# An odd-width shift, earlier softmax weights for the first batch, and projection steps under the last attention tiles

## The chip, the cores and the metric

The kernel runs on one core of one Trainium2 chip. The metric is the time of one execution on the device, in microseconds (us).

## The reference

A thresholded attention feeds a two-layer network:

```python
# q, k, v: (8 batches, 8 heads, 576 positions, 64); tau = 0.02
scores = scale * q @ k^T
thresh = max(scores, axis=-1) - tau
scores = where(scores >= thresh, scores, -1e9)
attn   = softmax(scores)                      # per row
x      = (attn @ v) -> (4608 tokens, 512)     # heads side by side
h      = x @ w_in                             # 512 -> 2048
out    = (h - tanh(h)) @ w_out                # 2048 -> 512, fp32
```

## The kernel before

The 64 heads are taken as 32 pairs. A pair is cut into 9 tiles of 128 query rows: A, B, A, B for the first head, a middle tile M with the last 64 rows of both heads, and A, B, A, B for the second. That makes 288 tiles, and the program is one loop over 288 **slots**. In slot s it starts the scores of tile s + 8, shifts the maxima of tile s + 7, bends tile s + 5, makes the softmax weights of tile s and multiplies tile s − 2 with v. The network's steps for the block of 512 tokens before ("h" for hidden, "y" for projection) are dealt out over the slots. Block 6 and 7 end in a tail after the last slot.

The parts that the change touches:

```python
def scores(i):
    ...  # matmuls into ps (ps_big, 2 buffers)
    if kind(j) == "B":
        mx = mxs[i] = mxs.pop(i - 1)          # B writes column 1 of A's tile
    else:
        mx = mxs[i] = st_pool.tile([P, 2], F32, name="mx", tag="mx")
    c = int(kind(j) == "B")
    nc.vector.tensor_scalar(                  # scale, evict, and row maximum
        out=sc, in0=ps[:, lo : lo + S], scalar1=SC, scalar2=None,
        op0=ALU.mult, op1=ALU.max, accum_out=mx[:, c : c + 1])

def shift(i):                                 # nb = tau - max, for A and B at once
    kd = kind(i % TPP)
    if kd == "A":
        return
    n = 2 if kd == "B" else 1
    mx = mxs.pop(i)
    nb = st_pool.tile([P, 2], F32, name="nb", tag="nb")
    nc.vector.tensor_scalar(
        out=nb[:, 0:n], in0=mx[:, 0:n], scalar1=-1.0, scalar2=tau,
        op0=ALU.mult, op1=ALU.add)
    ...
# kink(i):    ScalarE, z = Prelu(sc + nb) with a steep negative side
# weights(i): first batch: TensorE transposes z, ScalarE takes exp; later by DMA transposes
# attend(i):  TensorE, weights times v

def q_by_dma(p):                              # q of these pairs is transposed by DMA
    return p >= 2 * HPAIR and p % 2 == 1

def y_step(m, ms, part):                      # in layers(m, tail)
    if part == 0:
        odd = ms % 2
        pl, tag = (ps_o, "o") if tail and odd else (ps_y, "y")   # one buffer each
        ys[m, ms] = pl.tile(...), odd
    ps, odd = ys[m, ms]
    project(m, ms, part, ps, tail and odd)    # odd rows are emptied by ScalarE
```

GpSimd (POOL in the profile) splits q and k into two fp16 halves (`khl`, `qhl`), copies v and the weights, and swaps the halves of k (`kS`). Each of these instructions takes 0.3 to 1.3 us in the trace before (group means 0.29 to 1.28).

## Time and profile before

| | before |
|---|---|
| time, median of 3 runs | 544.43 us (544.36 to 545.31) |
| span of the profiled run | 542.9 us |
| until slot 37 or so (8 to 64 us) | POOL, ACT and DVE all near full |
| 64 to 138 us | DVE and ACT near full |
| 138 to 470 us | PE 97% busy |
| tail (470 us to the end) | PE alone |

The page's first row gives each engine's busy us, share and count of instructions:

```profile
PE 507.5 (93%) x4722; PEld 290.3 (53%) x4790; DVE 447.1 (82%) x1196; ACT 439.3 (81%) x630; POOL 290.7 (54%) x390
```

PE leads, but it can't gain on itself: what moves the end is idle time of PE, and who causes it. The prediction shows the stretches and lines that tell this.

### The profile page before, as it was taken

Reading aid. Unit: us, or ns where it says so; the run is one execution under the profiler, and the core shown is the slowest. Engines: PE = TensorE matmul, PEld = TensorE weight load, DVE = VectorE, ACT = ScalarE, POOL = GpSimd, SP = SyncE. Lnnn points to the kernel's source line nnn. Section 1 sums busy time; section 2 is a strip of 40 time slices with the busy share of each in tenths; the row PEclk is TensorE's granted clock in tenths of the full one; section 3 lists DMA queues with packets and bytes.
Section 4 is the critical chain, followed back from the end, with each engine's and each line's share of the span. In section 5 each row is a group of like instructions: output and inputs, shape, how many; then the busy total and the mean of one; then the engine's idle time right before and its main releaser. Section 6 shows DMA issues by size and latency. Waiting matters only on the chain.

```text
span 542.9 us, 12962 instructions
## 1 busy us (share of the span) xinstructions
PE 507.5 (93%) x4722; PEld 290.3 (53%) x4790; DVE 447.1 (82%) x1196; ACT 439.3 (81%) x630; POOL 290.7 (54%) x390
## 2 busy tenths in 40 slices
PE   5888888889999899999999999999999999899997
PEld 3566655555555555555555555555555555444444
DVE  4999999898888899889988989989989988544440
ACT  4899999998898888889888989899888989633330
POOL 7899987765456666557555755666655730000000
PEclk9999999998999999999999999999999999999999
DMA  7554688679697988789988999999999965310103
GB/s 211 168 182 145 205 202 175 148 131 197 141 173 160 175 169 199 163 191 195 181 188 172 177 200 186 165 171 191 192 177 179 200 127 117 83 41 39 40 39 77
DMA packets 202239, 85.13 MB, mean 157 GB/s; under 512 B 169792, under 2 KB 194624, under 8 KB 202176
## 3 DMA queue, kind: packets, MB, share of 16 engines
q1 hardware_dynamic: 201584, 83.89, 72.7%
q8 instruction: 37, 0.61, 0.5%
q10 hardware_dynamic: 592, 0.43, 0.3%
q14 instruction: 26, 0.21, 0.1%
HBM read 36.70 MB, written 9.44 MB: 85 GB/s over the span
## 4 chain that ended last, share of the span: by engine, by line
PE 67%; DVE 19%; POOL 6%; ACT 4%; issue 3%; DMA 0%; ACTq 0%; SPq 0%; DVEq 0%; POOLq 0%
PE psY L504 19%; PE psH L478 17%; PE psS L313 14%; DVE sc L323 9%; PE psO L423 5%; DVE g L497 3%; PE psS L303 3%; PE ps_k L227 3%; PE psHt L478 3%; DVE nb L337 2%; ACT z L357 2%; DVE osb L438 1%; POOL kS L256 1%; PE ps_q L227 1%; PE psO L412 1%
## 5 line engine op out<-in xcount | busy, mean ns | idle before, releaser
L323 DVE TENSOR_SCALAR_CACHE_REDUCE sc<-psS 128x576 f32<-128x576 f32 x288 | 215.3, 749 | 16.4 <-PE psS L313 11.0
L357 ACT ACTIVATE z<-sc,nb 128x576 bf16<-128x576 f32 x256 | 194.2, 771 | 21.9 <-DVE nb L337 21.3
L256 POOL COPY kS<-kT 64x1152 f16<-64x1152 f16 x62 | 70.9, 1143 | 135.8 <-DVE nb L337 133.2
L504 PE MATMUL psY<-w_out_sb,g 128*128 128x512 bf16 (+1 forms) x556 | 138.4, 373 | 2.2 <-issue 0.8
L394 ACT ACTIVATE pT<-zT 128x1152 f16<-128x1152 bf16 (+1 forms) x128 | 137.3, 1073 | 0.0
L478 PE MATMUL psH<-xT,w_in_sb 128*128 128x512 bf16 x451 | 118.0, 379 | 6.5 <-DVE g L497 4.4
L313 PE MATMUL psS<-kT,qT 128*128 128x512 f16 (+1 forms) x512 | 105.6, 288 | 11.2 <-DVE sc L323 9.2
L491 ACT ACTIVATE th<-psH 128x512 f32<-128x512 f32 x128 | 75.5, 590 | 39.2 <-PE psH L478 37.0
L313 PEld LDWEIGHTS <-qT 128*128 128x128 f16 x1024 | 73.1, 98 | 61.3 <-issue 14.5
L497 DVE SCALAR_TENSOR_TENSOR g<-th,psH 128x512 bf16<-128x512 f32 x128 | 87.2, 681 | 18.4 <-ACT th L491 18.4
L313 PE MATMUL psS<-kS,qT 128*128 128x512 f16 x496 | 101.9, 287 | 0.1
L478 PEld LDWEIGHTS <-w_in_sb 128*128 128x128 bf16 x576 | 49.4, 98 | 60.7 <-issue 7.2
L504 PEld LDWEIGHTS <-g 128*128 128x128 bf16 x592 | 51.0, 98 | 56.6 <-issue 2.9
L423 PEld LDWEIGHTS <-pT 128*128 128x128 f16 x1280 | 55.7, 98 | 25.0 <-issue 1.4
L423 PE MATMUL psO<-vb,pT 128*128 128x65 bf16 x1280 | 61.5, 194 | 0.9 <-ACT pT L394 0.6
L337 DVE TENSOR_SCALAR nb<-mx 128x2 f32<-128x2 f32 (+1 forms) x160 | 49.1, 307 | 2.5
L386 ACT ACTIVATE pT<-psZ 128x640 f16<-128x640 bf16 (+1 forms) x56 | 37.6, 671 | 5.1 <-PE psZ L377 5.0
L180 POOL TENSOR_TENSOR qhl<-qraw,qhl 128x576 f16<-128x576 f32 x31 | 39.7, 1281 | 2.6
L180 POOL TENSOR_TENSOR khl<-kraw,khl 128x576 f16<-128x576 f32 x31 | 39.7, 1281 | 2.6
L250 DVE COPY kT<-ps_k 128x1152 f16<-128x1152 f16 x31 | 23.4, 756 | 13.6 <-PE ps_k L227 13.2
L514 DVE COPY yo<-psY 128x512 f32<-128x512 f32 (+1 forms) x31 | 21.1, 679 | 11.3 <-PE psY L504 6.4
L438 DVE TENSOR_TENSOR osb<-psO,rc 128x256 bf16<-128x256 f32 x64 | 27.2, 424 | 2.2
(77 smaller groups left out, 508.4 us busy)
## 6 DMA issues: line engine op xcount, KB each, us to landing
vraw<-in_v_dram SPq DMA_DIRECT2D x32, 256.0 KB, 3.4
out_dram<-yo SPq DMA_DIRECT2D x32, 256.0 KB, 3.0
kraw<-in_k_dram SPq DMA_DIRECT2D x31, 256.0 KB, 3.2
qraw<-in_q_dram SPq DMA_DIRECT2D x31, 256.0 KB, 3.6
wt<-in_moe_w_in_dram SPq DMA_DIRECT2D x8, 512.0 KB, 4.7
wt<-in_moe_w_out_dram SPq DMA_DIRECT2D x8, 512.0 KB, 4.1
zT<-z SPq DMA_TRANSPOSE x104, 3.5
kraw<-in_k_dram SPq DMA_DIRECT2D x32, 32.0 KB, 2.8
```

Source lines behind the costliest of these rows:

```text
L180: nc.gpsimd.tensor_tensor(out=hl[:, :, 1, :], in0=x, in1=hl[:, :, 0, :], op=ALU.subtract)
L256: nc.gpsimd.tensor_copy(out=o, in_=i)
L313: nc.tensor.matmul(out=ps[:, dst], lhsT=lhs, rhs=kk[:, src], start=(n == 0), stop=(n == 1),)
L323: nc.vector.tensor_scalar(out=sc, in0=ps[:, lo : lo + S], scalar1=SC, scalar2=None, op0=ALU.mult, op1=ALU.max, accum_out=mx[:, c : c + 1],)
L337: nc.vector.tensor_scalar(out=nb[:, 0:n], in0=mx[:, 0:n], scalar1=-1.0, scalar2=tau, op0=ALU.mult, op1=ALU.add,)
L357: nc.scalar.activation(out=z, in_=sc, func=ACT.Prelu, bias=nb, scale=1.0, alpha=STEEP)
L394: nc.scalar.activation(out=pt[:, 0 : n * P], in_=zts.pop(i)[:, 0:n, :], func=ACT.Exp)
L423: nc.tensor.matmul(out=po[:, (j - 1 - 5 * hh) + ab, :], lhsT=pt[:, blk * P : (blk + 1) * P], rhs=vb[:, hh, c, :], start=(n == 0), stop=(n ...
L478: nc.tensor.matmul(out=ps, lhsT=w_in_sb[:, c, n * P : (n + 1) * P], rhs=xs[m][:, c, :] if m < B else xR[:, c, :, :], start=(c == 0), stop= ...
L491: nc.scalar.activation(out=th, in_=ps, func=ACT.Tanh)
L497: nc.vector.scalar_tensor_tensor(out=gs[m][:, n, :], in0=th, scalar=-1.0, in1=ps, op0=ALU.mult, op1=ALU.add,)
L504: nc.tensor.matmul(out=ps, lhsT=gs[m][:, n, ms * P : (ms + 1) * P], rhs=w_out_sb[:, n, cols], start=(n == 0), stop=(n == DF_C - 1),)
```

## The change

Its intent, as I read it: an element count of 3 in place of 2 should keep the shift from waiting for GpSimd. In the trace before, a shift of 128x2 takes 0.16 to 0.17 us where GpSimd is idle and up to 1.27 us where it starts inside a GpSimd instruction, and those over 230 ns end within 0.04 us of the end of one; this wait is called the lock below. For this the maxima move to six fixed tiles with a third, constant column. The weights of the first 36 tiles run four slots sooner. The q of pair 30 is transposed by DMA. Three projection steps of block 6 run in the three slots after the last one, where PE waits for the last attention tiles; odd rows of block 6 then share the other rows' accumulator, since the second one is still in use. The diff is cut; left out are lines that follow from these, and one in `ready` for block 0, which never asks it and so is not changed.

```diff
+    mx3 = []
+    for i in range(6):
+        mx = const.tile([P, 3], F32, name=f"mx{i}")
+        nc.vector.memset(mx, 0.0)
+        mx3.append(mx)
...
-        return p >= 2 * HPAIR and p % 2 == 1
+        return p >= 2 * HPAIR and (p % 2 == 1 or p == 30)
...
-            mx = mxs[i] = st_pool.tile([P, 2], F32, name="mx", tag="mx")
+            mx = mxs[i] = mx3[i // 2 % len(mx3)]
...
-        n = 2 if kd == "B" else 1
+        n = 3 if kd == "B" else 1
-        nb = st_pool.tile([P, 2], F32, name="nb", tag="nb")
+        nb = st_pool.tile([P, 3], F32, name="nb", tag="nb")
...
+    FIRST = 3
...
                 odd = ms % 2
+                odd = odd and m >= B - 1
...
                 not now or not ready(now[0]) or len(at) * ahead <= i * 16
-            ):
+            ) and not (m == B - 1 and i < FIRST):
...
+    for i in range(NTILE + 3):
+        at = i - 4 if i < HPAIR * TPP else i
+        atts.setdefault(at + LAG, []).append(i)
+        if i < NTILE:
+            wts.setdefault(at, []).append(i)
...
+        if s == NTILE:
+            todo = layers(stage, True)
+            share, done, stage = 1, 0.0, stage + 1
...
-        if 0 <= s < NTILE:
-            weights(s)
+        for i in wts.pop(s, []):
+            weights(i)
+        if 0 <= s < NTILE + FIRST:
...  (attend, norm and emit_x follow atts in the same way; the steps left over run after the loop)
```

More of the change, by code (lines that the diff above doesn't have):

```diff
@@ L340, in shift @@
         )
-        nbs[i] = nb[:, n - 1 : n]
+        nbs[i] = nb[:, n // 2 : n // 2 + 1]
         if kd == "B":
@@ L572, in ready @@
             last = 4 * y[2] + 3
-            return y[0] < m or len(at) > last and at[last] + 2 < i
+            return y[0] < m or len(at) > (last if m else 15) and at[last] + 2 < i
         while now or len(at) < 16:
@@ L658 @@
             plan.setdefault(-AHEAD, []).extend(plan.pop(at))
-    kinks = {}
-    for i in range(NTILE):
-        kinks.setdefault(i // 2 * 2 + 2 - AHEAD if i < 4 else i - MASK, []).append(i)
+    kinks, wts, atts = {}, {}, {}
+    for i in range(NTILE + 3):
[3 more added lines that the diff above has]
+            wts.setdefault(at, []).append(i)
+            kinks.setdefault(i // 2 * 2 + 2 - AHEAD if i < 4 else i - MASK, []).append(i)
     for s in range(-AHEAD, NTILE + LAG + 3):
@@ L679 @@
         bend()
-        if 0 <= s < NTILE:
-            weights(s)
+        for i in wts.pop(s, []):
+            weights(i)
+        if 0 <= s < NTILE + FIRST:
             if todo:
                 done += share
-                if j == TPP - 1 and p % HPAIR == HPAIR - 1:
+                if s < NTILE and j == TPP - 1 and p % HPAIR == HPAIR - 1:
                     done = 1e9
@@ L696 @@
         del stores[:-1]
-        if 0 <= s - LAG < NTILE:
-            attend(s - LAG)
-            pp, jj = divmod(s - LAG, TPP)
-            if jj == 4:
-                norm(pp, 0)
-            if jj == 8:
-                norm(pp, 1)
-        pp, jj = divmod(s - LAG, TPP)
-        if jj == 1 and 0 < pp <= NPAIR:
-            emit_x(pp - 1)
+        for i in atts.pop(s, []):
+            pp, jj = divmod(i, TPP)
+            if i < NTILE:
+                attend(i)
+            if i < NTILE and jj in (4, 8):
+                norm(pp, int(jj > 4))
+            if jj == 1 and pp:
+                emit_x(pp - 1)
         for step in plan.pop(s, []):
@@ L715 @@
                     w_load(piece)
+    for step in todo:
+        step()
+        bend()
+        shrink()
+        for store in stores:
+            store()
+        stores.clear()
     while stage < NMB:
```

## The prediction

If the lock is dodged, 6.4 + 0.2 + 0.6 − 0.4 = 6.8 us less than 544.4, thus 537.6 us; if not, without the 6.4, 0.4 us less, thus 544.0 us.

> **What bounds the kernel now.** I read the page first, then the stretches of the trace by busy time, then the chain of waits, then single lines. The program has no single bound, so I cut it into stretches. The columns are the stretch in us, its length, then busy us (and instructions) of PE, PEld, DVE, ACT and POOL, the granted clock, the DMA share and GB/s:
>
> ```profile
> 8.00:64.00 56.00, 49.19 (x651) 34.74 (x649) 51.08 (x145) 48.83 (x80) 52.10 (x65) 1.00 0.59 181
> 64.00:138.00 74.00, 65.27 (x714) 40.88 (x721) 68.39 (x183) 67.64 (x101) 54.24 (x69) 0.98 0.81 168
> 138.00:470.00 332.00, 323.03 (x3006) 180.72 (x3057) 297.36 (x817) 296.69 (x408) 178.81 (x229) 1.00 0.88 174
> 470.00:543.00 73.00, 67.37 (x341) 32.27 (x343) 27.77 (x44) 23.15 (x39) 0.00 (x0) 1.00 0.14 44
> ```
>
> From 138 us on PE is busy 323.03 of 332 us: only PE work, or its 9 us of idle time, can be won there. From 64 to 138 us DVE (68.39 of 74) and ACT (67.64) are near full together. Before 64 us POOL is as full as DVE, and the chain of waits stays on POOL from 37.3 to 73.3 us. Three of its pieces (start, us, what), and the wait of PE that proves POOL the limit in this stretch:
>
> ```profile
> 61.01 1.04 POOL w_out_sb L605
> 62.11 1.15 POOL kS L256
> 63.30 1.16 POOL kS L256
> ```
>
> ```profile
> 37.33 1.28 POOL L180 TENSOR_TENSOR qhl<-qraw,qhl 128x576 f16<-128x576 f32 x1
> 38.67 0.68 PE L227 MATMUL ps_q<-ident_f,qhl 128*128 128x128 f16 x9 [1.10 <-POOL qhl L180]
> ```
>
> The q transposes start 0.06 us after POOL ends qhl. I paired every POOL product with its first use on PE: the slack is 0.06 to 0.54 us for the k and q of head pairs 2 to 5, and the kS of pair 5 ends at 64.44 us where PE uses it. It is 2.9 us and more for pair 6 and later. POOL's gaps from 17 to 73 us are the 40 to 90 ns between any two of its instructions. So up to 64 us the clock of the program is POOL's work list, which the change does not shorten.
>
> Now the line that the change aims at. The two groups of the shift (count | busy us, mean ns | idle before), then two places where it ran long:
>
> ```profile
> L337 DVE TENSOR_SCALAR nb<-mx 128x2 f32<-128x2 f32 x128 | 44.4, 347 | 2.5
> L337 DVE TENSOR_SCALAR nb<-mx 128x1 f32<-128x1 f32 x32 | 4.6, 144 | 0.0
> ```
>
> ```profile
> 122.31 1.28 POOL L180 TENSOR_TENSOR khl<-kraw,khl 128x576 f16<-128x576 f32 x1
> 122.34 1.27 DVE L337 TENSOR_SCALAR nb<-mx 128x2 f32<-128x2 f32 x1
> ...
> 274.58 1.28 POOL L180 TENSOR_TENSOR qhl<-qraw,qhl 128x576 f16<-128x576 f32 x1
> ...
> 274.85 1.03 DVE L337 TENSOR_SCALAR nb<-mx 128x2 f32<-128x2 f32 x1
> ...
> 277.80 1.02 PE L478 MATMUL psH<-xT,w_in_sb 128*128 128x512 bf16 x4 [0.67 <-DVE g L497]
> ```
>
> Two elements per partition cost 1.27 and 1.03 us, and each ends within 0.03 us of the end of the POOL instruction beside it. I went through all 160: every 128x2 one over 230 ns does so, the rest lie at 142 to 230 ns, and no 128x1 one is ever long, even when it starts inside a POOL instruction. The last line shows what it can cost: the first hidden-layer matmul of a block waits 0.67 us because the copies ahead of its operand on DVE were late.
>
> [...] the trace holds no odd width but 1 and can't say. This is my largest doubt. [...] the large sc evictions, which read PSUM, do last about 0.75 us with or without POOL at work beside them.
>
> **The change part by part.**
> 1. Odd width (2 becomes 3, the maxima in six fixed tiles). If it dodges the lock, 128 × (347 − 144) = 26.0 us of DVE waiting goes. By stretch, from busy time of that line less 144 ns each: 8.54 − 24 × 0.144 = 5.1 us before 64 us; 10.89 − 27 × 0.144 = 7.0 us from 64 to 138; 29.62 − 111 × 0.144 = 13.6 us from 138 to 470. Before 64 us POOL paces the program, so I count 0.4 us (the one real POOL gap, 1.04 us at 16.2 us, waits for a DVE copy that stands behind a 0.63 us shift). From 64 to 138 us the 7.0 us leave DVE at 61.4 busy, and ACT with 67.6 of 74 becomes the next bound: I count 3 us. From 138 us most of it becomes DVE idle time. PE's waits there for DVE are 3.0 (psH for g) + 1.6 (psS for sc) + 0.5 (xT) + 0.2 = 5.3 us; I count 3 us. Sum 6.4 us. Six more memsets at about 0.1 us lie in the first 4 us, where DVE waits for the first load.
> 2. Softmax weights four slots sooner for the first 36 tiles: nothing is added or removed. Four exponentials of about 0.6 us (0.612 and 0.716 mean) move into ACT's idle time at 13.9, 17.4 and 19.0 us (1.04, 1.45 and 0.82 us), so ACT, which lags by about 3 us until 40 us, leads sooner. But POOL paces these slots and slot 37 comes at 64 us either way. The first hidden-layer step comes at the same slot. I count 0.2 us.
> 3. q of pair 30 turned by DMA: 9 transposes leave PE, 20.64 us / 279 = 0.074 us each, 0.67 us, in a stretch where PE sets the pace; I count 0.6 us. A DVE copy of 0.75 us goes too. The DMA takes about 3.4 us to land, and DMA load falls just there because loads end.
> 4. Three projection steps (12 matmuls, 3 × 0.86 us) under the last attention tiles. PE idles there now:
>
> ```profile
> 470.79 0.49 PE L423 MATMUL psO<-vb,pT 128*128 128x65 bf16 x10 [0.57 <-ACT pT L394]
> ...
> 472.02 0.40 PE L455 MATMUL psX<-ident_bf,osb 128*128 128x128 bf16 x4 [0.74 <-DVE osb L438]
> ```
>
> These 1.3 us would be filled. Against it: block 6 now keeps one accumulator tile, where odd rows had another one, and ACT to empty it. The first two steps meet at a row change at once, a wait for the copy of about 0.85 us (0.69 us and the handing over). Later at three row changes one hidden step of 0.86 us stands between, while DVE first finishes g (0.69) and then copies yo (0.69): some 0.4 us each. Sum: 1.3 − 0.85 − 1.2 = −0.7; some overlap is likely, so I count −0.4 us.
>
> If the lock is dodged: 6.4 + 0.2 + 0.6 − 0.4 = 6.8 us less, 537.6 us. If not: 0.4 us less, 544.0 us.
>
> **Rivals.** (a) [...] Then the shift stays at about 350 ns and the time at 544. [...] Against it: a width of 1 is never held, and such care for a width (a third, constant column) makes sense only if it works. I give it 35%. (b) The lock goes, but ACT or the DMA transposes take over at once: ACT is at 91% from 64 to 138 us, and one PE wait of 1.46 us at 122.1 us is for a q transpose by DMA. Then only 3 us come, 541. (c) The held DVE was the hidden pacemaker: each hold also delays evictions, and so PE, beyond the named waits (nb holds 10 us, 1.9%, of the chain of waits), and the sooner weights help more than I allow. Then 10 to 12 us, 533. (d) The single accumulator costs more than the filled idle time: 1 us more at the end.
>
> **Range and chances.** 65% at about 537.6 (535 to 541) and 35% at about 544 (543 to 545) put the middle near 538.5. Eight in ten: 533.5 to 544.8. Faster by over 2% means below 533.5 us, thus (c): 10%. Slower by 2% would need a new stall of 11 us, for which I see no source: 2%.
>
> **What would show it.** The shift's group as 128x3 with a mean near 150 ns (lock dodged) or near 350 (not). Slot 37, PE's first use of pair 5's kS, still at 64 us within 1 us. The stretch after it some 3 us shorter, with ACT fuller than DVE. The 0.67 us waits before psH gone. At the end, the two waits of 0.57 and 0.74 us gone and new waits of psY for the yo copy. I am wrong if the time to 64 us falls by more than 1 us, if the shift is short and the time stays above 541, or if PE's transposes or the loads get a new wait.

## The result

The kernel after takes 547.54 us (median of 6 runs, 546.08 to 547.75) against 544.65 us (6 runs) for the kernel before on the same chip. The ratio is 1.0046, with a 95% interval of 1.0032 to 1.0060. Ratios here are the mean time of one kernel's fast runs over that of the other's of the same rounds, so they are not quite the ratio of the medians quoted. The kernel is a little slower, outside the predicted range of 533.5 to 544.8 us.

The shift's groups in the kernel after (count | busy us, mean ns | idle before):

```profile
L343 DVE TENSOR_SCALAR nb<-mx 128x3 f32<-128x3 f32 x128 | 45.0, 351 | 2.4
L343 DVE TENSOR_SCALAR nb<-mx 128x1 f32<-128x1 f32 x32 | 4.6, 145 | 0.0
```

Three wide takes 351 ns on average where two wide took 347. The lock is still there. But that explains only why nothing was won, not a loss. The same stretches as before, and one longer at the end:

```profile
8.00:64.00 56.00, 50.39 (x670) 34.95 (x669) 52.48 (x150) 50.40 (x82) 52.99 (x66) 1.00 0.61 187
64.00:138.00 74.00, 65.12 (x714) 40.50 (x725) 67.30 (x184) 68.33 (x101) 56.08 (x72) 1.00 0.78 167
138.00:470.00 332.00, 318.38 (x2957) 177.49 (x3007) 297.08 (x806) 294.04 (x403) 176.86 (x226) 1.00 0.86 174
470.00:546.00 76.00, 70.02 (x357) 33.32 (x361) 30.62 (x50) 23.63 (x39) 0.00 (x0) 1.00 0.14 42
```

Fixed clock times compare different work once one kernel is ahead, so I cut the traces by work instead: from the first score eviction to the 91st ("head"), to the 280th ("body"), and from there to the end.

| profiled run | first eviction at | head | body | end | span |
|---|---|---|---|---|---|
| before | 8.52 us | 129.60 | 308.89 | 95.94 | 542.9 |
| after | 8.71 us | 127.08 | 313.45 | 96.52 | 545.8 |

The head is 2.5 us shorter, the end 0.6 us longer, and the body, which no part of the change was meant to touch, **4.6 us longer**. PE does the same work there (300.75 and 300.61 us busy within these bounds); its idle time grew. What PE waited for, in us in total, times, and the longest, from 138 us on: first before, then after (there to 473 us):

```profile
PE psH L478 <- DVE g L497: 3.0, 5, 0.7
...
PE psS L313 <- DVE sc L323: 1.6, 5, 0.7
...
PE psH L478 <- DVE xT L468: 0.5, 1, 0.5
```

```profile
PE psS L319 <- DVE sc L329: 4.6, 9, 1.3
PE psH L484 <- DVE g L503: 2.7, 5, 0.7
PE psH L484 <- DVE xT L474: 2.5, 5, 0.5
```

PE waits more for DVE. To find why, I followed DVE in step through both traces. Where both are in the same rhythm, a shift of the one stays at a constant distance from the same shift of the other, except at one place in each even head pair, where the kernel after loses 0.22 us. DVE at that place in pair 16, before and after:

```profile
238.97 0.14 DVE L337 TENSOR_SCALAR nb<-mx 128x1 f32<-128x1 f32 x1
239.03 0.75 DVE L323 TENSOR_SCALAR_CACHE_REDUCE sc<-psS 128x576 f32<-128x576 f32 x1
```

```profile
236.68 0.15 DVE L343 TENSOR_SCALAR nb<-mx 128x1 f32<-128x1 f32 x1
236.96 0.76 DVE L329 TENSOR_SCALAR_CACHE_REDUCE sc<-psS 128x576 f32<-128x576 f32 x1
```

The eviction that follows M's shift starts 0.06 us after the shift's start in the kernel before, and 0.28 us after it in the kernel after. The list of instructions says why. Columns: place, line, operation, tiles, engines waited for:

```
421 L343 TensorScalarPtr nb<-mx_99 128x1 [waits DVE_49]
422 L329 TensorScalarPtr sc,mx_99<-psS 128x576 [waits DVE_49,PE_49]
```

The two use one tile, mx_99. The new index is `i // 2`. In an even pair M is tile 4 and the next A is tile 5 of the pair, counted from an even number, so both give the same index. The eviction of A now writes into the tile that M's shift has just read, and must wait for that shift to end. The kernel after has 16 evictions with such a wait on their own engine, the kernel before none; in its trace they start 0.27 to 0.31 us after the start of M's shift in all 16 even pairs, against 0.06 us in 14 of them before.

Four slots later in the same pair, before and after, this is what the step does:

```profile
243.61 0.66 POOL L179 CAST khl<-kraw 128x576 f16<-128x576 f32 x1
...
244.18 0.17 DVE L337 TENSOR_SCALAR nb<-mx 128x2 f32<-128x2 f32 x1
...
244.36 1.28 POOL L180 TENSOR_TENSOR khl<-kraw,khl 128x576 f16<-128x576 f32 x1
```

```profile
242.07 1.28 POOL L186 TENSOR_TENSOR khl<-kraw,khl 128x576 f16<-128x576 f32 x1
242.14 1.23 DVE L343 TENSOR_SCALAR nb<-mx 128x3 f32<-128x3 f32 x1
```

Before, the shift starts 0.09 us ahead of the end of GpSimd's cast and is out after 0.17 us. After, it comes 0.07 us behind the start of the next, longer instruction and is held for 1.23 us. A step of 0.22 us became 1.06 us more.

At the tail, the waits of PE named in the prediction are gone and the feared ones are there: 0.78 us at the first row change, and three more of 0.28 us. The first of them:

```profile
474.11 1.02 PE L510 MATMUL psY<-w_out_sb,g 128*128 128x512 bf16 x4 [0.78 <-DVE yo L520]
```

### The profile page after: what moved, and what is told of

The parts are those of the page before. It is cut to its first block, busy times and chain, and to the rows that moved or that the text cites. A ratio compares the mean times of both kernels' runs of the same rounds, so it can differ in the third digit from the quotient of the medians.

```text
span 545.8 us, 12963 instructions
## 1 busy us (share of the span) xinstructions
PE 506.3 (93%) x4713; PEld 287.9 (53%) x4781; DVE 449.9 (82%) x1203; ACT 439.4 (81%) x628; POOL 291.0 (53%) x390
## 4 chain that ended last, share of the span: by engine, by line
PE 65%; DVE 23%; ACT 5%; issue 4%; DMA 2%; SPq 0%; DVEq 0%; ACTq 0%
PE psY L510 18%; PE psH L484 16%; PE psS L319 14%; DVE sc L329 11%; PE psO L429 5%; DVE g L503 4%; PE psS L309 3%; PE ps_k L233 3%; DVE nb L343 2%; ACT z L363 2%; PE psHt L484 2%; DVE yo L520 2%; ACT pT L392 2%; DVE osb L444 1%; PE psO L418 1%
## 5 line engine op out<-in xcount | busy, mean ns | idle before, releaser
L343 DVE TENSOR_SCALAR nb<-mx 128x3 f32<-128x3 f32 (+1 forms) x160 | 49.6, 310 | 2.4
L520 DVE COPY yo<-psY 128x512 f32<-128x512 f32 (+1 forms) x33 | 22.5, 680 | 12.1 <-PE psY L510 7.6
```

The lines of the kernel that those rows point to most:

```text
L343: nc.vector.tensor_scalar(out=nb[:, 0:n], in0=mx[:, 0:n], scalar1=-1.0, scalar2=tau, op0=ALU.mult, op1=ALU.add,)
```

## The experiments

My theory S: the shared tile of maxima costs the body its time, by itself and by moving DVE onto longer holds of GpSimd. Rivals: W, the width itself costs; N, the body's pattern is a matter of chance and any change in the head can upset it. For each run I give the time, the ratio to the kernel before of the same rounds, and the lengths from its one trace. The diffs are cut to the lines that matter. "Hold" is what shifts in the body last beyond 170 ns each, summed: 11.54 us before, 14.68 us after.

### p1_odd: part 1 alone, as in the diff

```diff
-            mx = mxs[i] = st_pool.tile([P, 2], F32, name="mx", tag="mx")
+            mx = mxs[i] = mx3[i // 2 % len(mx3)]
-        n = 2 if kd == "B" else 1
+        n = 3 if kd == "B" else 1
```

> The kernel before with part 1 alone, as in the diff (three-wide shift, maxima in six fixed tiles taken by i // 2). Theory S (the fixed tiles make the middle tile M and the next tile A of each even head pair share one tile of maxima, so that 16 evictions wait for the shift before them, 0.22 us each, and the DVE falls behind GpSimd by that step): slower, 546.5 to 549 us, 16 evictions with a DVE wait, body (138 to 470 us of before) some 3 to 5 us longer. Theory W (the width itself costs): slower too, but then the next run, p1_apart, is as slow. Theory N (the body depends on chance of timing from the head alone): same as before, 544.6.

548.56 us, ratio 1.0057 (1.0038 to 1.0075). Body 312.41 us, hold 13.58 us, 16 evictions with the wait. Part 1 by itself accounts for the whole loss (1.0046 in the kernel after); what the other parts win back is within the intervals.

### p1_apart: part 1 with a tile of its own for M

```diff
-            mx = mxs[i] = mx3[i // 2 % len(mx3)]
+            mx = mxs[i] = mx3[(5 * (i // TPP) + (j + 1) // 2) % len(mx3)]
```

> As p1_odd, but the six tiles are taken in turn by group, so that M and A never share one. Theory S: 544.6 us within 0.7, no eviction waits for a shift, the shift as 128x3 still about 350 ns mean (the lock stays). Theory W: as slow as p1_odd, 546.5 or more. If three wide dodged the lock after all, the mean would be near 150 ns and the time 538.

545.65 us, ratio 1.0007 (0.9994 to 1.0019): as before. (This is 1.0 us above the 544.6 expected, but the kernel before stood at 545.2 in these rounds.) Body 308.92 us, hold 11.53 us, no eviction with the wait. The same place in pair 16:

```profile
237.95 0.14 DVE L343 TENSOR_SCALAR nb<-mx 128x1 f32<-128x1 f32 x1
238.01 0.75 DVE L329 TENSOR_SCALAR_CACHE_REDUCE sc<-psS 128x576 f32<-128x576 f32 x1
```

The step back to 0.06 us takes the loss away with the width left at 3. W falls. The shift as 128x3 takes 346 ns here, so a width of 3 is neither a help nor a harm.

### p1_share2: the shared tiles, two wide

```diff
+        mx = const.tile([P, 2], F32, name=f"mx{i}")
-            mx = mxs[i] = st_pool.tile([P, 2], F32, name="mx", tag="mx")
+            mx = mxs[i] = mx3[i // 2 % len(mx3)]
```

> The kernel before with the six fixed tiles and their sharing, but the shift left two wide. Theory S: slower like p1_odd, within 0.7 us of it. Theory W: 544.6.

546.98 us, ratio 1.0035 (1.0016 to 1.0055). Body 311.08 us, hold 12.30 us. The sharing costs without the width. The time is 1.6 us below p1_odd's, where at most 0.7 us was expected; the two intervals overlap, so this gap is not shown to be a real one.

Where the body loses its time can be read pair by pair, from the start of M's shift against the same shift before. By the M of the next pair, each of the three kernels with the sharing has made the 0.22 us good within 0.04 us after the even pairs 10, 12, 14, 18, 22 and 26. The loss comes after pairs 16, 20, 24 and 28, where the kernel before has no long hold (none of its shifts there is over 0.31 us):

| | after pairs 16, 20, 24, 28 | sum | body longer by |
|---|---|---|---|
| p1_share2 | 0.53, 0.53, 0.53, 0.53 us | 2.1 | 2.2 |
| p1_odd | 0.52, 0.52, 0.54, 1.87 us | 3.4 | 3.5 |
| kernel after | 1.87, 0.54, 0.53, 1.87 us, and 0.40 won back after pair 29 | 4.4 | 4.6 |

With about 0.53 us one shift is held 0.67 to 0.68 us, with 1.87 us two are held 1.23 and 0.8 us, where each took 0.17 us before. So the waits as such cost the body next to nothing. They cost by moving shifts onto longer holds of GpSimd: S is right in its second half only. Which hold is met differs between kernels that share the tile alike, so N has a share in the size, but not in the cause.

### after_apart: the kernel after, with a tile of its own for M

The edit of p1_apart, on the kernel after.

> The kernel after, whole, but with the tiles of maxima taken by group (no sharing). Theory S: the body goes back to what before needs, and the 2.3 us won in the head stay: 542 to 544 us. Theory W or N: stays near 547.5 us.

543.98 us, ratio 0.9974 (0.9962 to 0.9986). Body 308.55 us, hold 11.60 us. One index takes the kernel after from 0.46% slower to 0.26% faster than before. So the shared tile is the cause of the loss in the whole kernel too, and not only in part 1.

### p2_sooner: the earlier weights alone

```diff
+        at = i - 4 if i < HPAIR * TPP else i
-            weights(s)
+        for i in wts.pop(s, []):
+            weights(i)
```

> The kernel before with the softmax weights of the first 36 tiles four slots sooner and nothing else. The head pair 5 starts its scores 2.0 us sooner in the kernel after (64.77 for 66.75 us), pair 10 2.3 us sooner. Theory S (the body's loss is from the shared tiles): 542.3 us, all of the head's gain kept. Theory N (any shift of phase in the head upsets the body): 544 to 547 us. My prediction's step (POOL paces the head, 0.2 us): 544.4 us.

543.8 us, ratio 0.9975 (0.9955 to 0.9994), so some 1.4 us less (0.3 to 2.5). That is more than the 0.2 us of the prediction, and less than the 2.3 us that S had expected (542.3 us). Body 308.83 us: N would have had the body upset by the part, and it is not. The head is 128.04 against 129.60 us, but this alone shows little: heads without the part differ by 1.3 us between traces (129.60 before, 128.26 in p1_share2). What the part changes in the head is shown at pair 5, below.

### p4_tail: the steps under the last attention tiles alone

```diff
+                odd = odd and m >= B - 1
+            ) and not (m == B - 1 and i < FIRST):
+        if s == NTILE:
+            todo = layers(stage, True)
```

> The kernel before with block 6's three projection steps under the last attention tiles and nothing else. From the trace of after: idle PE of 0.57 and 0.74 us goes, waits of psY for yo of 0.78 and 3 times 0.28 us come: 0.33 us slower, 545.0 us. If the filled time were worth more than the waits, faster.

545.91 us, ratio 1.0012 (0.9993 to 1.0031). By the trace, PE's waits of 0.57 and 0.74 us are gone, those of 0.78 and three of 0.28 us are there, and the end is 96.59 against 95.94 us, 0.65 us longer. The ends of the ten traces without the part lie between 95.87 and 95.95 us, those of the three with it between 96.52 and 96.61. So the part is a small loss in the traces, and unclear in the times.

### p3_q30: the q of pair 30 by DMA alone

```diff
-        return p >= 2 * HPAIR and p % 2 == 1
+        return p >= 2 * HPAIR and (p % 2 == 1 or p == 30)
```

> The kernel before with q of pair 30 turned by DMA and nothing else. 9 transposes less on PE, 0.67 us, in a stretch where PE is the bound: 544.0 us if nothing else moves; up to 1 us slower if the phase between DVE and GpSimd or the landing of the transpose upsets pairs 29 to 31.

544.67 us, ratio 0.9987 (0.9969 to 1.0004): unclear, at most a little faster. In its trace the body is 309.01 us, no shorter than before. PE's 0.67 us of transposes turned into a new wait of 0.66 us, at the first scores of pair 30:

```profile
431.83 0.36 PEld L313 LDWEIGHTS <-qT 128*128 128x128 f16 x4 [1.15 <-DMA qT<-qhl]
431.83 0.42 PE L313 MATMUL psS<-kT,qT 128*128 128x512 f16 x2 [0.66 <-DVE nb L337]
```

The view puts the matmul's wait down to a shift on DVE, which these scores don't use. Its weights wait for the transposed q: the DMA is issued at 428.43 us and lands at 431.79, and both instructions start 0.04 us later. So the wait is for the transpose itself.

### shift_ones: two shifts of one column

```diff
-        nc.vector.tensor_scalar(out=nb[:, 0:n], in0=mx[:, 0:n], ...)
+        for c in range(n):
+            nc.vector.tensor_scalar(out=nb[:, c : c + 1], in0=mx[:, c : c + 1], ...)
```

> The kernel before with the shift of two maxima done as two instructions of one column each. [...] no shift is over 200 ns and the 26 us of DVE waiting are replaced by 128 more instructions of 144 ns (18 us, less where they overlap). Lock theory: body's PE waits for DVE (0.67 us before psH once a batch, 0.2 us) go, and the time is 540 to 543 us. If the lock's cost lay off the critical path: 544.6 or slower, since DVE has more instructions.

538.61 us, ratio 0.9884 (0.9863 to 0.9904). This is the experiment that measures what the lock costs, in a kernel that does the same arithmetic:

```profile
L338 DVE TENSOR_SCALAR nb<-mx 128x1 f32<-128x1 f32 x288 | 35.7, 148 | 0.0
```

```profile
117.79 0.29 POOL L212 CAST vb<-vraw 64x128 bf16<-64x128 f32 x1
117.85 0.21 DVE L338 TENSOR_SCALAR nb<-mx 128x1 f32<-128x1 f32 x2
```

None of the 288 is over 156 ns, also when it starts inside a GpSimd instruction; two in a row take 0.21 us. The head is 124.64 us (5.0 less than before) and the body 307.04 us (1.9 less). The gain is 1.16%, 6.3 us (5.2 to 7.5), more than the expected 540 to 543 us would have been.

### share_ones: shared tiles, two shifts of one column

The edits of p1_share2 and of shift_ones together.

> The kernel before with the six shared tiles of maxima and the shift done as one-column instructions: the added wait of 16 evictions without the lock. If that wait costs by itself (0.22 us at each even pair, DVE short of time), 1 to 3.5 us slower than shift_ones (538.6), thus 539.6 to 542. If it costs only by moving DVE onto a longer hold of GpSimd, as slow as shift_ones, 538.6 within 0.7.

539.73 us, ratio 0.9894 (0.9879 to 0.9910), against 0.9884 (0.9863 to 0.9904) for shift_ones in other rounds. The time by itself lies in the first expected range, but the kernel before stood 0.7 us higher here (545.62 against 544.96), and by the ratios the two are not told apart. Body 307.12 against 307.04 us: without the lock the 16 waits are not seen to cost the body anything, which agrees with the account by pairs under p1_share2. The head is 0.9 us longer (125.58); why stays open.

### shift_nine: nine columns in, three rows of three out

```diff
+            dst, src = nb[:, :, 0:3], mx[:, 0:9].rearrange("p (a b) -> p a b", a=3)
+        nc.vector.tensor_scalar(out=dst, in0=src, ...)   # nb is [P, 3, 4]: a gap in each row
```

Two outcomes were expected: first that this shape is not held, then that it is.

> The kernel before with the shift reading nine columns and writing three rows of three with a gap between rows, tiles of maxima apart. [...] shift near 150 to 170 ns in all cases, time 538 to 540 us. [...] the mean stays near 350 ns and the time near 544.9.

538.84 us, ratio 0.9879 (0.9866 to 0.9893).

```profile
L347 DVE TENSOR_SCALAR nb<-mx 128x9 f32<-128x9 f32 x128 | 20.3, 159 | 2.5
```

The longest of them is 165 ns: no hold at all, in one instruction. The trace gives the count of elements alone, so how the source was encoded, and why this shape is free where 128x3 is held, stays open.

### best_no_tail and best_tail_alt: the parts that paid, together

Both have one-column shifts with the tiles of the kernel before, the earlier weights and the q of pair 30 by DMA. The second adds the steps under the last attention tiles, with only row 2 of block 6 in the second accumulator:

```diff
-                odd = ms % 2
+                odd = ms == 2 if tail and m < B - 1 else ms % 2
```

> The kernel before with one-column shifts, weights four slots sooner and q of pair 30 by DMA, without the change at the tail: shift_ones (6.3 us less), p2_sooner (1.2 us less) and p3_q30 (0.3 to 0.7 us less) added: 536.5 to 538 us.

> As best_no_tail, with the three projection steps under the last attention tiles, but rows 2 of block 6 in the second accumulator and emptied by ACT: of the waits of psY for yo only the one of 0.78 us and one of 0.28 us should stay, against 1.30 us of idle time that goes: 0.2 us faster than best_no_tail. If the tail's cost is not those waits, 0.3 us or more slower than best_no_tail.

best_no_tail: 539.18 us, ratio 0.9879 (0.9866 to 0.9893). best_tail_alt: 538.66 us, ratio 0.9879 (0.9860 to 0.9897). Neither is told apart from shift_ones (0.9884) and shift_nine (0.9879) by its interval, and the expectation of 536.5 to 538 us was a miss: the parts do not add. With the lock gone, the earlier weights win nothing (head 126.20 us against 124.64 in shift_ones). Pair 5 starts at 55.3 us after the first eviction in shift_ones and at 55.4 us in best_no_tail, and in both the first matmul that needs its kS starts 0.05 us after GpSimd has made it. Before, this slack was 0.98 us; each of the two parts takes it away alone, so they win the same time up to there. Why the head is longer after that is open. In best_tail_alt the waits of psY are the expected 0.78 and 0.28 us and the end is 95.66 us, the expected 0.2 us less than the 95.87 without; the times don't tell the two apart.

## Why the prediction was wrong

**The odd width: the step "If it dodges the lock", given 65%, failed.** Rival (a) was right on the shift: three to three is held as two to two is. (Its time of 544 us was not met, since the next point came on top.) 128x3 lasts 351 ns on average and up to 1.28 us, 128x2 347 ns and up to 1.27 us, and p1_apart shows that the width changes nothing. I trusted the care of the edit more than a doubt that the trace before did not settle: it holds no odd width but 1.

**A step that was missing: "the maxima in six fixed tiles" was costed at six memsets.** It made M and A share a tile in even pairs, hence 16 waits, 0.22 us each. These moved shifts onto longer holds of GpSimd, up to two in place of none in a pair, and that is the whole of the miss above 544.0 us: without the sharing the kernel after takes 543.98 us. The diff shows it in `i // 2`, and the instruction list with its waits showed it before any run. I looked at that list only for the order.

**The value of the lock, 6.4 us, was right as a sum, in part by luck.** shift_ones gains 6.3 us. The split was not right: I counted 0.4 us before 64 us, 3 up to 138 and 3 after. Measured are 5.0 us in the head as a whole and 1.9 in the body. Within the head, pair 5's first eviction follows GpSimd's kS by 2.31 us before and by 0.59 us in shift_ones, 1.7 us less, and the way from there to the 91st eviction is 2.0 us shorter. The step that counted too little before 64 us is that of the next point.

**Earlier weights: 0.2 us counted, 1.4 measured (0.3 to 2.5).** The failing step is "the kS of pair 5 ends at 64.44 us where PE uses it", and with it "POOL paces these slots". The first matmul that waits for this kS starts at 65.42 us in the kernel before, 0.98 us after GpSimd is done; I had taken the next use of any kS, which was pair 4's. In the kernel after it starts 0.12 us after GpSimd. Before and after:

```profile
62.11 2.33 POOL L256 COPY kS<-kT 64x1152 f16<-64x1152 f16 x2
...
65.42 0.41 PE L313 MATMUL psS<-kS,qT 128*128 128x512 f16 x2
```

```profile
61.77 2.33 POOL L262 COPY kS<-kT 64x1152 f16<-64x1152 f16 x2
...
64.23 0.41 PE L319 MATMUL psS<-kS,qT 128*128 128x512 f16 x2
```

This slack is 0.98 us in all six traces with two or three wide shifts and without the earlier weights, and 0.07 to 0.12 us in the three with them. The shift just ahead of pair 5's first eviction is held for 1.0 us in the six and takes 0.22 us at most in the three. So this eviction starts at 64.77 us in the kernel after instead of 66.75. That it was ACT's load of four exponentials in these slots that had kept PE behind GpSimd is my reading; no run tests it. The prediction's own sign of this error came true: PE's first use of pair 5's kS moved by 1.2 us, more than the 1 us allowed.

**The q of pair 30: 0.6 us counted, 0 in the trace.** The prediction named the 3.4 us that the DMA takes to land, but its sum took them as hidden. They are not: PE waits 0.66 us for the landing in p3_q30, the new wait at the transposes that the prediction had named as a sign of being wrong. The times allow anything from 1.7 us less to 0.2 us more.

**The tail: −0.4 us counted, and the waits are those foretold.** The first was sized at 0.85 us and is 0.78, the later ones at 0.4 and are 0.28; the idle time that they replace is 1.30 us, so the waits alone come to −0.33 us and the length of the end to −0.65 us.

## What to carry to other kernels

When tiles from a rotating pool become fixed tiles picked by an index, list who gets which tile and compare the waits of each instruction before and after: a write that now waits for the last reader on the same engine (here it started 0.28 us after that reader's start in place of 0.06) is easy to miss, since no line of the diff says that it waits. A tiny DVE instruction beside a busy GpSimd is to be judged by its longest cases, not by its mean (1.27 us against 0.35 here), and written in a form that the trace shows is not held; one column at a time, never over 156 ns, was enough here, worth 1.2%. Small waits in such a pair of engines can be amplified by the next hold (here 0.22 us became 1.06 us more), so try each part of a change alone.
